# The last 64 rows of w_down: 25 partitions with three rows each in place of 128 half rows

## The chip, the cores and the metric

The kernel runs on one core of a Trainium2 chip. The metric is device time in microseconds (us), the median over runs of the whole program. A profile is one more execution; it has a time of its own and a span, from the first to the last instruction that it records.

## The reference

One token passes through a transformer block: attention over a cache of 4096 positions with 32 heads of 128, then a gated feed-forward layer. Everything is bf16 at the borders.

```python
h  = x + A(layernorm(x))        # q = ln @ wq; softmax(q k^T / sqrt(128)) v; @ wo
g  = ln2 @ w_gate               # ln2 = layernorm(h), 640 -> 1728
u  = ln2 @ w_up
h2 = h + (gelu_tanh(g) * u) @ w_down   # 1728 -> 640
```

The change touches only the last product. 1728 is 13 * 128 + 64, so 13 full slices of 128 rows of `w_down` leave a remainder of 64 rows.

## The kernel before, in words

**Order of work.** A small class `S` collects the instructions of each engine in program order; every engine runs its own list in order, and an instruction waits on semaphores of what it needs. There is no scheduler: the order in the source is the order on the engine. All large transfers are issued by SyncE (SP) on one queue, in source order: `wq`, the K and V caches in 16 pieces of 4 MB, `wo` in two parts, `w_gate`, `w_up`, and last the pieces of `w_down`. So the queue holds work from the start to the end.

**Attention.** Eight groups of four heads: VectorE (DVE) multiplies K by the broadcast q (L329), TensorE (PE) folds the products (L338), DVE and ScalarE (ACT) make the softmax, and PE multiplies by V (L385, and L393 for the last group). The projection by `wo` is L586.

**Feed-forward.** `up` (L632) makes g in PSUM tile `pg` and u in `pu`, each 128 partitions by `NF` = 14 columns. Columns 0 to 12 hold the 13 full slices. Column 13 holds rows 1600 to 1727 on partitions 0 to 127: its upper 64 partitions are the remaining rows 1664 to 1727, its lower 64 repeat rows that are already in another column. DVE and ACT compute the gelu (L639 to L647), and L648 writes `hm`, bf16, 128 by 14.

**The down product.** `w_down` lies in `wd_sb`, by slots of 640 columns. It comes in five transfers, issued in this order: `wdr`, the remainder, into slot 13 (L566); then `wd0` to `wd3` (L571) with 6, 4, 2 and 1 slots, 128 partitions each. Each output of 640 is cut into four quarters, `j`, which are accumulated on four rows (0, 32, 64, 96) of PSUM tile `pd` (shown as `pf` in the profile), so one slot is four matmuls of one column of `hm` (the stationary operand) by 160 columns of `wd_sb` (L664). PE goes through the slots of `wd0`, then slot 13, then `wd1`, `wd2`, `wd3`; before the first matmul of each it waits for that transfer. L668 copies `pd` to SBUF, and L669 stores it.

**The remainder before.** Row r of the 64 is cut in halves: half h lies on partition 2r + h, so slot 13 has 128 partitions of 320 columns. To match this, one matmul (L650) with the selection matrix `twice` copies h of row r to partitions 2r and 2r + 1, and DVE (L652) multiplies by the parity mask `hpar`, which gives two columns `hr`: one is zero on odd partitions, the other on even ones. Quarters 0 and 1 use the first column, quarters 2 and 3 the second. `hpar` and `twice` are made at the start by DVE (L219, L221) from the identity `I32`.

Of the kernel before, what the change touches and what calls it, by code (L numbers as in the profile page):

```python
# [5 lines left out]
FP32 = mybir.dt.float32  # L6
BF16 = mybir.dt.bfloat16
ALU = mybir.AluOpType
ACTF = mybir.ActivationFunctionType
AX = mybir.AxisListType  # L10

D = 640
# [3 lines left out]
DF = 1728  # L16
NC_D = D // 128
# [6 lines left out]
NG = H // HG  # L24
# [9 lines left out]
NFT = 13  # L34
NF = NFT + 1
WD_PARTS = (6, 4, 2, 1)

WD_COLS = []
for _n in WD_PARTS:
    _b = 128 * len(WD_COLS)  # L40
    WD_COLS += [(_b, _n, _i) for _i in range(_n)]
FREM = DF - NFT * 128


class Sched:
# [64 lines left out]
def bass_sequential_preLN__gqa_block_cached__glu_gated_geglu__decode_kernel(  # L110
# [12 lines left out]
    S = Sched(nc)  # L123

    def sb(name, shape, dt):
        return nc.alloc_sbuf_tensor(name, shape, dt)
# [5 lines left out]
    vbuf = [sb("vbuf%d" % i, [128, R, DH], BF16) for i in range(2)]  # L132

    def over(name, base, shape):
        return nc.alloc_sbuf_tensor_at(name, shape, BF16, offset=nc.lookup_mloc(base).addr)
# [2 lines left out]
    wo_sb = over("wo_sb", arena, [128, NW, HW, D])  # L138
    wg_sb = over("wg_sb", kbuf[NG % 2], [128, NC_D, DF])
    wu_sb = over("wu_sb", kbuf[(NG + 1) % 2], [128, NC_D, DF])  # L140
    wd_sb = over("wd_sb", vbuf[NG % 2], [128, NF, D])

    NPR = 3
    prod = [sb("prod%d" % i, [128, RP, DH], BF16) for i in range(NPR)]
# [33 lines left out]
    r_t = sb("r_t", [128, NF], FP32)  # L178
    gu = sb("gu", [128, NF], FP32)
    hm = sb("hm", [128, NF], BF16)  # L180
    hr = sb("hr", [128, 2], BF16)
    hpar = sb("hpar", [128, 2], FP32)
    twice = sb("twice", [128, FREM, 2], BF16)
    o_sb = sb("o_sb", [128, D // 4], BF16)
    hx = sb("hx", [128, 32, NC_D], FP32)
    m32 = sb("m32", [128, 32], FP32)
# [5 lines left out]
    I32 = sb("I32", [128, 128], FP32)  # L192
# [5 lines left out]
    pz = nc.alloc_psum_tensor("pz", [128, 512], FP32)  # L198
# [17 lines left out]

    t_e4 = S.op("vector", lambda v: v.reduce_sum(
        e4[:, :], I32[:, :].rearrange("p (j i) -> p j i", j=4), axis=AX.X), [t_i32])
    S.op("vector", lambda v: v.reduce_sum(  # L219
        hpar[:, :], I32[:, :].rearrange("p (r h) -> p h r", h=2), axis=AX.X))  # L220
    t_tw = S.op("vector", lambda v: v.tensor_copy(  # L221
        twice[:, :, :], I32[:, 128 - FREM:128].unsqueeze(2).to_broadcast([128, FREM, 2])))
    t_m32 = S.op("vector", lambda v: v.reduce_sum(
        m32[:, :], I32[:, :].rearrange("p (j i) -> p i j", j=4), axis=AX.X))
    S.op("vector", lambda v: v.reduce_sum(
# [3 lines left out]
    a = S.op("vector", lambda v: v.reduce_sum(  # L229
        jred[:, :], I32[:, :].rearrange("p (j c) -> p j c", c=HW), axis=AX.X))  # L230
    b = S.op("vector", lambda v: v.reduce_sum(
        cred[:, :], I32[:, :].rearrange("p (j c) -> p c j", c=HW), axis=AX.X))
# [11 lines left out]
    kfree, vfree = [None] * NG, [None] * NG  # L244
# [45 lines left out]
    a = None  # L290
    for c in range(NC_D):
        a = S.op("tensor", lambda t, c=c: t.matmul(
            pm[:, c:c + 1], x_sb[0:1, c::NC_D], ones_bf[0:1, 0:1],
            start=(c == 0), stop=(c == NC_D - 1), skip_group_check=True),
            [d_x, t_onebf], token=(c == NC_D - 1))
# [146 lines left out]
    for n in range(NG - 1):  # L442
        w = (n - 3) // 2 if n >= 3 and n % 2 else None
        p, o = n - 1, n - 2
# [62 lines left out]
    p, o = g - 1, g - 2  # L507
# [45 lines left out]
    def load_wo(lo, hi):  # L553
# [10 lines left out]
    d_wu = pieces("wu", wu_sb, B_w_up[:, :].rearrange("(p c) n -> p c n", c=NC_D),  # L564
                  [0, 5], [kfree[NG - 1]])
    d_wdr = S.dma("sync", "wdr", lambda s: s.dma_start(  # L566
        wd_sb[:, NFT, 0:D // 2], B_w_down[NFT * 128:DF, :].rearrange("r (h n) -> (r h) n", h=2)), [vfree[NG - 2]])
    d_wd = []
    for i, n in enumerate(WD_PARTS):
        s0 = len(d_wd)  # L570
# [1 line left out]
            wd_sb[:, s0:s0 + n, :],  # L572
            B_w_down[128 * s0:128 * (s0 + n), :].rearrange("(p i) n -> p i n", i=n)), [vfree[NG - 2]])
        d_wd += [tok] * n
    d_wd.append(d_wdr)


    pp = pf[0]
# [1 line left out]
    def project(w):  # L580
        tok = None
        for c in range(HW):
            for cc in range(NC_D):
                last = w == NW - 1 and c == HW - 1 and cc == NC_D - 1
                first = w == 0 and c == 0 and cc == 0
                tok = S.op("tensor", lambda t, c=c, cc=cc, first=first, last=last: t.matmul(  # L586
                    pp[:, cc:cc + 1], wo_sb[:, w, c, cc::NC_D], aP[:, w * HW + c:w * HW + c + 1],
                    start=first, stop=last, skip_group_check=True),
                    [t_aP[w], d_wo[w], red_done[NG * NP - 2]], token=last)
        return tok  # L590

    for i in range(w - 1):
# [8 lines left out]
    b = project(w)  # L601
    t_h = S.op("vector", lambda v: v.scalar_tensor_tensor(
        out=h32[:, :], in0=x32[:, :], scalar=1.0, in1=pp[:, 0:NC_D], op0=ALU.mult, op1=ALU.add,
# [4 lines left out]
    NQ = D // 4  # L608
# [13 lines left out]
    def up(ps, w, d_w):  # L622
# [16 lines left out]
    a = S.op("vector", lambda v: v.tensor_copy(g_t[:, :], pg[:, 0:NF]), [t_g])  # L639
    a = S.op("vector", lambda v: v.tensor_mul(t1[:, :], g_t[:, :], g_t[:, :]), [a])  # L640
    a = S.op("vector", lambda v: v.tensor_mul(t2[:, :], t1[:, :], g_t[:, :]), [a])
    a = S.op("vector", lambda v: v.scalar_tensor_tensor(
        out=t3[:, :], in0=t2[:, :], scalar=GELU_C1, in1=g_t[:, :], op0=ALU.mult, op1=ALU.add), [a])
    a = S.op("scalar", lambda a: a.activation(e_t[:, :], t3[:, :], ACTF.Exp, scale=-2.0 * GELU_C0), [a])
    a = S.op("vector", lambda v: v.tensor_scalar(d_t[:, :], e_t[:, :], 1.0, 0.0, ALU.add, ALU.add), [a])
    a = S.op("vector", lambda v: v.reciprocal(r_t[:, :], d_t[:, :]), [a])
    a = S.op("vector", lambda v: v.tensor_mul(gu[:, :], g_t[:, :], r_t[:, :]), [a])  # L647
    t_hm = S.op("vector", lambda v: v.tensor_mul(hm[:, :], gu[:, :], pu[:, 0:NF]), [a, t_u])  # L648

    b = S.op("tensor", lambda t: t.matmul(  # L650
        pz[:, 32:33], twice[:, :, :], hm[:, NFT:NF], start=True, stop=True), [t_hm, t_tw])
    t_hr = S.op("vector", lambda v: v.tensor_tensor(  # L652
        out=hr[:, :], in0=hpar[:, :], in1=pz[:, 32:33].to_broadcast([128, 2]), op=ALU.mult), [b])

    def down(s, j):
        if s == NFT:
            return hr[:, j // 2:j // 2 + 1], wd_sb[:, NFT, j % 2 * NQ:(j % 2 + 1) * NQ]
        return hm[:, s:s + 1], wd_sb[:, s, j * NQ:(j + 1) * NQ]

    order = list(range(WD_PARTS[0])) + [NFT] + list(range(WD_PARTS[0], NFT))  # L660
    for i, s in enumerate(order):
        for j in range(4):
            last = i == NF - 1
            b = S.op("tensor", lambda t, s=s, j=j, last=last: t.matmul(  # L664
                pd[32 * j:32 * j + 1, 0:NQ], *down(s, j),
                start=False, stop=last, skip_group_check=True),
                [t_hr if s == NFT else t_hm, d_wd[s]], token=(last and j == 3))
    t_o = S.op("vector", lambda v: v.tensor_copy(o_sb[:, :], pd[:, 0:NQ]), [b])  # L668
    d_o = S.dma("sync", "out", lambda s: s.dma_start(  # L669
        out[0, 0, :].rearrange("(j i) -> j i", j=4), o_sb[0:128:32, :]), [t_o])  # L670
# [32 lines left out]
```

## Time and profile before

| what | value |
|---|---|
| median of 3 runs | 203.93 us (203.84 to 203.95) |
| the profiled execution | 204.04 us |
| its span | 202.8 us |
| PE busy | 154.4 us (76%) |
| DVE busy | 116.0 us (57%) |
| read from HBM | 84.23 MB, 415 GB/s over the span |
| share of the 16 DMA engines' time in the main queue | 97.2% |
| `hm` ready (end of L648) | 198.15 us |
| first and last matmul of the down product begin | 198.32 and 200.41 us |
| copy of the result begins (L668) | 200.77 us |

Times inside the execution are microseconds from the start of its span. The trace also holds, for each transfer, the landing records: a transfer over 128 partitions runs on all 16 DMA engines, and each engine reports its own share by one increment of the transfer's semaphore. And it holds the packets, with start, duration and size, though not the number of the DMA engine that carried each.

### The profile page before, as it was taken

The page shows a single profiled execution, that of the slowest core. Times are in us where ns is not written, and L with a number is a line of the kernel's source. Part 1 is how long each engine was busy: PE and PEld are TensorE (multiplying, and loading weights), DVE is VectorE, ACT ScalarE, POOL GpSimd, SP SyncE. Part 2 cuts the span into 40 slices and gives each one's busy share as a digit, 9 for nine tenths or more (in the row PEclk, how much of TensorE's full clock was granted, in tenths as well). Part 3 has the DMA queues.
Part 4 walks back from the last instruction along what each step waited for, and adds up shares of the span by engine and source line. Part 5 has one row for each costly group of instructions (what it writes and reads, how often), then busy time and mean ns, then how long its engine had stood idle before and what let it go on. Part 6 is the DMA issues. An engine that isn't in the chain of part 4 may idle for free.

```text
span 202.8 us, 2488 instructions
## 1 busy us (share of the span) xinstructions
PE 154.4 (76%) x1074; PEld 71.5 (35%) x1080; DVE 116.0 (57%) x150; ACT 30.6 (15%) x110; POOL 1.2 (1%) x7
## 2 busy tenths in 40 slices
PE   1005348689959967998899499959876999988685
PEld 1001013233324322442343134313422344587483
DVE  6100087998099628883993599268899524311121
ACT  2002200006003300240060006000602204000000
POOL 1000000000000000000000000000000000000000
PEclk9999999999999996999999999988999999975555
DMA  7999999999999999999999999999999999999992
GB/s 251 444 436 414 414 472 452 414 420 414 436 465 433 420 409 420 449 448 420 433 414 427 456 427 433 427 414 433 459 427 430 387 424 468 433 393 430 410 404 85
DMA packets 4020, 84.38 MB, mean 416 GB/s; under 512 B 425, under 2 KB 682, under 8 KB 1066
## 3 DMA queue, kind: packets, MB, share of 16 engines
q1 hardware_dynamic: 4008, 84.23, 97.2%
q8 instruction: 8, 0.13, 0.3%
q14 instruction: 2, 0.02, 0.0%
q10 hardware_dynamic: 2, 0.00, 0.0%
HBM read 84.23 MB, written 0.00 MB: 415 GB/s over the span
## 4 chain that ended last, share of the span: by engine, by line
DMA 58%; DVE 24%; PE 15%; SPq 1%; issue 1%
DMA kbuf<-in_A_k_cache_dram 47%; DVE prod L329 17%; DMA wd_sb<-in_B_w_down_dram 11%; PE pf L338 6%; PE pg L385 4%; DVE sc L345 4%; PE pu L385 4%; DVE xz L402 2%; DVE xm L399 1%; SPq L571 0%; DVE mx L353 0%; PE pf L664 0%; DVE mrow L362 0%; PE pm L357 0%; SPq L237 0%
## 5 line engine op out<-in xcount | busy, mean ns | idle before, releaser
L329 DVE TENSOR_TENSOR prod<-kbuf,qb 128x4096 bf16<-128x4096 bf16 x32 | 72.8, 2278 | 46.6 <-DMA kbuf<-in_A_k_cache_dram 46.6
L338 PE MATMUL pf<-prod,Ibf 128*128 128x512 bf16 x256 | 66.0, 405 | 24.4 <-DVE prod L329 24.4
L338 PEld LDWEIGHTS pf<-prod,Ibf 128*128 128x128 bf16 x256 | 24.2, 103 | 63.2 <-DVE prod L329 31.0
L385 PE MATMUL pg<-vbuf,P 128*16 128x512 bf16 x128 | 30.0, 379 | 0.0
L345 DVE TENSOR_REDUCE sc<-pf 128x32 f32<-128x512 f32 x32 | 21.7, 677 | 4.7 <-PE pf L338 4.7
L385 PE MATMUL pu<-vbuf,P 128*16 128x512 bf16 x96 | 22.2, 379 | 0.0
L308 PE MATMUL pq<-wq_sb,xb 128*128 128x512 bf16 x34 | 10.8, 451 | 13.6 <-DMA wq_sb<-in_A_wq_dram 11.6
L370 ACT ACTIVATE nb<-pm 128x4 f32<-128x4 f32 x8 | 1.4, 173 | 119.7 <-PE pm L367 119.7
L374 ACT ACTIVATE P<-sc,nb 32x128 bf16<-32x128 f32 x32 | 18.5, 578 | 0.9
L385 PEld LDWEIGHTS pg<-vbuf,P 128*16 128x16 bf16 x128 | 10.6, 89 | 14.5 <-issue 1.3
L385 PEld LDWEIGHTS pu<-vbuf,P 128*16 128x16 bf16 x96 | 8.1, 90 | 11.7 <-issue 1.7
L314 ACT CAST qb<-pq 32x128 bf16<-32x128 f32 x32 | 8.2, 256 | 16.3 <-PE pq L308 15.6
L308 PEld LDWEIGHTS pq<-wq_sb,xb 128*128 128x128 bf16 x40 | 3.8, 110 | 17.6 <-issue 13.3
L374 ACT ACTIVATION_READ_ACCUMULATOR P<-sc,nb 32x1 f32 x32 | 8.0, 251 | 0.0
L586 PE MATMUL pf<-aP,wo_sb 128*128 128x1 bf16 x160 | 7.0, 178 | 1.3 <-issue 1.0
L586 PEld LDWEIGHTS pf<-aP,wo_sb 128*128 128x128 bf16 x160 | 6.8, 131 | 1.9 <-issue 1.5
L402 DVE TENSOR_REDUCE xz<-xm 16x128 f32<-16x512 f32 x7 | 7.3, 1038 | 0.2
L399 DVE TENSOR_TENSOR xm<-pg,rmask 16x512 f32<-16x512 f32 x4 | 2.7, 671 | 3.4 <-PE pg L385 3.4
L393 PE MATMUL pq<-P,vbuf 128*128 128x4 bf16 x128 | 3.6, 166 | 0.6 <-DMA vbuf<-in_A_v_cache_dram 0.6
L283 ACT ACTIVATE ln<-pz,ln 128x1 f32<-128x1 f32 x2 | 0.5, 261 | 23.2 <-DVE ln L280 23.2
L399 DVE TENSOR_TENSOR xm<-pu,rmask 16x512 f32<-16x512 f32 x3 | 1.9, 644 | 3.2 <-PE pu L385 3.2
L393 PEld LDWEIGHTS pq<-P,vbuf 128*128 128x128 bf16 x128 | 3.5, 104 | 0.7 <-DMA vbuf<-in_A_v_cache_dram 0.7
(80 smaller groups left out, 56.1 us busy)
## 6 DMA issues: line engine op xcount, KB each, us to landing
kbuf<-in_A_k_cache_dram SPq DMA_DIRECT2D x8, 4096.0 KB, 25.1
vbuf<-in_A_v_cache_dram SPq DMA_DIRECT2D x8, 4096.0 KB, 22.7
wq_sb<-in_A_wq_dram SPq DMA_DIRECT2D x1, 5120.0 KB, 15.4
wo_sb<-in_A_wo_dram SPq DMA_DIRECT2D x1, 3840.0 KB, 27.2
wg_sb<-in_B_w_gate_dram SPq DMA_DIRECT2D x1, 2160.0 KB, 21.5
wu_sb<-in_B_w_up_dram SPq DMA_DIRECT2D x1, 2160.0 KB, 26.2
wo_sb<-in_A_wo_dram SPq DMA_DIRECT2D x1, 1280.0 KB, 16.8
wd_sb<-in_B_w_down_dram SPq DMA_DIRECT2D x1, 960.0 KB, 21.4
```

The costliest lines, as they stand in the source:

```text
L308: tok = S.op("tensor", lambda t, c=c, n0=n0: t.matmul(pq[:, :], xb[:, c, :], wq_sb[:, c, n0:n0 + HG * DH], start=(c == 0), stop=(c == NC_D ...
L314: t_qb[g] = S.op("scalar", lambda a, lo=lo, hi=hi, hh=hh: a.copy(qb[lo:hi, g, :], pq[lo:hi, hh * DH:(hh + 1) * DH]), [tok])
L329: return S.op("vector", lambda v: v.tensor_tensor(out=prod[n % NPR][:, :, :], in0=kbuf[g % 2][:, s * RP:(s + 1) * RP, :], in1=qb[:, g, :]. ...
L338: fold_done[n] = S.op("tensor", lambda t, j=j: t.matmul(pf[n % 2][:, :], Ibf[:, :], prod[n % NPR][:, :, j * W:(j + 1) * W], start=(j == 0) ...
L345: red_done[n] = S.op("vector", lambda v: v.reduce_sum(sc[g % 2][:, s * RP:(s + 1) * RP], pf[n % 2][:, :].rearrange("p (r w) -> p r w", r=R ...
L370: e = S.op("scalar", lambda a: a.activation(nb[:, g * HG:(g + 1) * HG], pm[:, 256:256 + HG], ACTF.Copy, scale=-SCALE), [d])
L374: t_exp[g] = S.op("scalar", lambda a, lo=lo, hi=hi, h=h, hh=hh: a.activation(P4[g % 2][lo:hi, :, hh], sc[g % 2][lo:hi, :], ACTF.Exp, bias= ...
L385: t_pv[g] = S.op("tensor", lambda t, i=i, r=r, last=last: t.matmul(pv[g % 2][0:VM, :], P4[g % 2][:, r:r + VR, :], vbuf[g % 2][:, r:r + VR, :],
L393: t_pv[g] = S.op("tensor", lambda t, r=r: t.matmul(pq[:, 0:HG], vbuf[g % 2][:, r, :], P4[g % 2][:, r, :], start=(r == 0), stop=(r == R - 1 ...
L399: a = S.op("vector", lambda v: v.tensor_tensor(out=xm[:, :, :], in0=pv[g % 2][0:VM, :].rearrange("p (r d) -> p r d", r=VR), in1=rmask[:, : ...
L402: t_ext[g] = S.op("vector", lambda v: v.reduce_sum(xz[g % 2][:, :], xm[:, :, :].rearrange("p r d -> p d r"), axis=AX.X), [a, t_acc[g - 2] ...
L586: tok = S.op("tensor", lambda t, c=c, cc=cc, first=first, last=last: t.matmul(pp[:, cc:cc + 1], wo_sb[:, w, c, cc::NC_D], aP[:, w * HW + c ...
```

## The change

The remainder is now read as 75 whole rows, 1653 to 1727, with three rows of 640 columns on each of 25 partitions; rows 1653 to 1663 are read a second time, and their h is set to zero. `wd_sb` has 16 slots, 13 to 15 being the remainder. `hq` is column 13 of `hm` spread over three columns by the mask `hcol` (1 where the row's place among the 75, modulo 3, is the column's number, and 0 on the lower 64 partitions); one matmul with the selection matrix `hrow` sums it to 25 partitions by three columns, and DVE copies that to `hr`. PE goes through the slots of `wd0` and `wd1`, then 13 to 15, then `wd2` and `wd3`.

```diff
+NRP = 25
+NRR = 3
+ROFF = 128 - NRP * NRR
...
-    S.op("vector", lambda v: v.reduce_sum(
-        hpar[:, :], I32[:, :].rearrange("p (r h) -> p h r", h=2), axis=AX.X))
-    t_tw = S.op("vector", lambda v: v.tensor_copy(
-        twice[:, :, :], I32[:, 128 - FREM:128].unsqueeze(2).to_broadcast([128, FREM, 2])))
+    hsum = hx[:, 0:NRP // NC_D, :]
+    t_hsum = S.op("vector", lambda v: v.reduce_sum(
+        hsum, I32[:, ROFF:128].rearrange("p (a b i) -> p a b i", b=NC_D, i=NRR), axis=AX.X))
+    t_hrow = S.op("vector", lambda v: v.memset(hrow[:, :], 0.0))
+    t_hrow = S.op("vector", lambda v: v.tensor_copy(
+        hrow[:, 0:NRP].rearrange("p (a b) -> p a b", b=NC_D), hsum), [t_hsum, t_hrow])
+    t_hcol = S.op("vector", lambda v: v.reduce_sum(
+        hcol[:, :], I32[:, ROFF:128].rearrange("p (r i) -> p i r", i=NRR), axis=AX.X))
+    t_hcol = S.op("vector", lambda v: v.memset(hcol[0:128 - FREM, :], 0.0), [t_hcol])
...
     d_wdr = S.dma("sync", "wdr", lambda s: s.dma_start(
-        wd_sb[:, NFT, 0:D // 2], B_w_down[NFT * 128:DF, :].rearrange("r (h n) -> (r h) n", h=2)), [vfree[NG - 2]])
+        wd_sb[0:NRP, NFT:NFT + NRR, :],
+        B_w_down[DF - NRP * NRR:DF, :].rearrange("(p i) n -> p i n", i=NRR)), [vfree[NG - 2]])
...
+    a = S.op("vector", lambda v: v.tensor_tensor(
+        out=hq[:, :], in0=hcol[:, :], in1=hm[:, NFT:NF].to_broadcast([128, NRR]), op=ALU.mult), [t_hm, t_hcol])
     b = S.op("tensor", lambda t: t.matmul(
-        pz[:, 32:33], twice[:, :, :], hm[:, NFT:NF], start=True, stop=True), [t_hm, t_tw])
-    t_hr = S.op("vector", lambda v: v.tensor_tensor(
-        out=hr[:, :], in0=hpar[:, :], in1=pz[:, 32:33].to_broadcast([128, 2]), op=ALU.mult), [b])
+        pz[:, 32:32 + NRR], hrow[:, :], hq[:, :], start=True, stop=True), [a, t_hrow])
+    t_hr = S.op("vector", lambda v: v.tensor_copy(hr[:, :], pz[:, 32:32 + NRR]), [b])

     def down(s, j):
-        if s == NFT:
-            return hr[:, j // 2:j // 2 + 1], wd_sb[:, NFT, j % 2 * NQ:(j % 2 + 1) * NQ]
+        if s >= NFT:
+            return hr[0:NRP, s - NFT:s - NFT + 1], wd_sb[0:NRP, s, j * NQ:(j + 1) * NQ]
         return hm[:, s:s + 1], wd_sb[:, s, j * NQ:(j + 1) * NQ]

-    order = list(range(WD_PARTS[0])) + [NFT] + list(range(WD_PARTS[0], NFT))
+    n = sum(WD_PARTS[0:2])
+    order = list(range(n)) + list(range(NFT, NFT + NRR)) + list(range(n, NFT))
```

More of the change, by code (lines that the diff above doesn't have):

```diff
@@ L140, in bass_sequential_preLN__gqa_block_cached__glu_gated_geglu__decode_kernel @@
     wu_sb = over("wu_sb", kbuf[(NG + 1) % 2], [128, NC_D, DF])
-    wd_sb = over("wd_sb", vbuf[NG % 2], [128, NF, D])
+    wd_sb = over("wd_sb", vbuf[NG % 2], [128, NFT + NRR, D])
     NPR = 3
@@ L180, in bass_sequential_preLN__gqa_block_cached__glu_gated_geglu__decode_kernel @@
     hm = sb("hm", [128, NF], BF16)
-    hr = sb("hr", [128, 2], BF16)
-    hpar = sb("hpar", [128, 2], FP32)
-    twice = sb("twice", [128, FREM, 2], BF16)
+    hq = sb("hq", [128, NRR], BF16)
+    hr = sb("hr", [128, NRR], BF16)
+    hcol = sb("hcol", [128, NRR], FP32)
+    hrow = sb("hrow", [128, 128], BF16)
     o_sb = sb("o_sb", [128, D // 4], BF16)
@@ L574, in bass_sequential_preLN__gqa_block_cached__glu_gated_geglu__decode_kernel @@
         d_wd += [tok] * n
-    d_wd.append(d_wdr)
+    d_wd += [d_wdr] * NRR
     pp = pf[0]
@@ L648, in bass_sequential_preLN__gqa_block_cached__glu_gated_geglu__decode_kernel @@
     t_hm = S.op("vector", lambda v: v.tensor_mul(hm[:, :], gu[:, :], pu[:, 0:NF]), [a, t_u])
+    a = S.op("vector", lambda v: v.tensor_tensor(
+        out=hq[:, :], in0=hcol[:, :], in1=hm[:, NFT:NF].to_broadcast([128, NRR]), op=ALU.mult), [t_hm, t_hcol])
     b = S.op("tensor", lambda t: t.matmul(
-        pz[:, 32:33], twice[:, :, :], hm[:, NFT:NF], start=True, stop=True), [t_hm, t_tw])
-    t_hr = S.op("vector", lambda v: v.tensor_tensor(
-        out=hr[:, :], in0=hpar[:, :], in1=pz[:, 32:33].to_broadcast([128, 2]), op=ALU.mult), [b])
+        pz[:, 32:32 + NRR], hrow[:, :], hq[:, :], start=True, stop=True), [a, t_hrow])
+    t_hr = S.op("vector", lambda v: v.tensor_copy(hr[:, :], pz[:, 32:32 + NRR]), [b])
     def down(s, j):
-        if s == NFT:
-            return hr[:, j // 2:j // 2 + 1], wd_sb[:, NFT, j % 2 * NQ:(j % 2 + 1) * NQ]
+        if s >= NFT:
+            return hr[0:NRP, s - NFT:s - NFT + 1], wd_sb[0:NRP, s, j * NQ:(j + 1) * NQ]
         return hm[:, s:s + 1], wd_sb[:, s, j * NQ:(j + 1) * NQ]
-    order = list(range(WD_PARTS[0])) + [NFT] + list(range(WD_PARTS[0], NFT))
+    n = sum(WD_PARTS[0:2])
+    order = list(range(n)) + list(range(NFT, NFT + NRR)) + list(range(n, NFT))
     for i, s in enumerate(order):
         for j in range(4):
-            last = i == NF - 1
+            last = i == len(order) - 1
             b = S.op("tensor", lambda t, s=s, j=j, last=last: t.matmul(
@@ L666, in bass_sequential_preLN__gqa_block_cached__glu_gated_geglu__decode_kernel @@
                 start=False, stop=last, skip_group_check=True),
-                [t_hr if s == NFT else t_hm, d_wd[s]], token=(last and j == 3))
+                [t_hr if s >= NFT else t_hm, d_wd[s]], token=(last and j == 3))
     t_o = S.op("vector", lambda v: v.tensor_copy(o_sb[:, :], pd[:, 0:NQ]), [b])
```

## The prediction

> **What bounds the kernel now.** I read the page's slices and queues first, then the end of the chain of waits, then the timeline of the last five microseconds, then DMA in that window.
>
> ```profile
> PEclk9999999999999996999999999988999999975555
> DMA  7999999999999999999999999999999999999992
> q8 instruction: 8, 0.13, 0.3%
> ```
>
> DMA is full in all slices but the first and last: the kernel is a stream of weights and cache, and what counts is when its last bytes land and what follows. PE's granted clock is 0.5 in the last four slices. The eight instruction packets of q8 matter below.
>
> ```profile
> 176.66 0.43 SPq L571
> 177.09 0.04 issue
> 177.13 22.85 DMA wd_sb<-in_B_w_down_dram
> 199.99 0.04 issue
> 200.03 0.71 PE pf L664 x9
> ```
>
> The chain ends in `wd2` landing at 199.99 and the last matmuls. In the timeline, the last waits:
>
> ```profile
> 197.98 0.17 DVE L648 TENSOR_TENSOR hm<-gu,pu 128x14 bf16<-128x14 f32 x1 [1.80 <-PE pu L632]
> 198.20 0.10 PEld L650 LDWEIGHTS pz<-hm,twice 128*128 128x128 bf16 x1 [0.42 <-DVE hm L648]
> 198.32 0.97 PE L664 MATMUL pf<-wd_sb,hm 128*1 128x160 bf16 x24
> 199.08 0.34 PE L664 MATMUL pf<-wd_sb,hr 128*1 128x160 bf16 x4
> 199.21 1.50 PE L664 MATMUL pf<-wd_sb,hm 128*1 128x160 bf16 x28
> 200.03 0.10 PEld L664 LDWEIGHTS pf<-wd_sb,hm 128*1 128x1 bf16 x8 [0.41 <-DMA wd_sb<-in_B_w_down_dram]
> 200.41 0.09 PEld L664 LDWEIGHTS pf<-wd_sb,hm 128*1 128x1 bf16 x4 [0.28 <-DMA wd_sb<-in_B_w_down_dram]
> ```
>
> PE idles twice, for `wd2` and for `wd3` (which landed at 200.37); everything after 200.41 (four matmuls, copy, store) is fixed. So a single number decides: when the last four matmuls can begin. It is the later of the last share of `wd3` and of PE's own queue.
>
> **The landing.** Stretching 195 to 203 us into 40 slices of 0.2 us shows that the 16 engines do not end together:
>
> ```profile
> DMA  9899899889999989665543100000000000000000
> ```
>
> The landing records of `wd3` give each engine's end: 198.35, .40, .47, .57, .58, .75, .97, then 199.35, .47, .72, .82, .88, .93, .95, 200.13 and 200.37. In the packet records an engine runs its packets back to back (each starts within some 10 ns of another's end, so that 16 chains can be followed), and it gets the same share of every transfer, so a delay stays: a q8 packet of 16 KB holds one engine for 1.02 to 1.10 us, its next packet is about 0.5 us slow, and each time another engine is hit. Seven of the nine late engines carry such a hit.
>
> **The change, part by part.**
>
> *Removed from the queue:* `wdr` before is 8 packets of 640 B on each of 16 engines; its landings stand 0.20 to 0.23 us behind those of `w_up`, engine by engine. That goes from every engine that gets no share of the new one: 0.21.
>
> *Added:* 25 packets of 3840 B (25 contiguous pieces on both sides). Packets of 2560 and 5120 B take 0.102 and 0.198 us here, so one takes 0.15. How 25 packets spread isn't shown. In every transfer of this trace the engines used carry equal shares (128 partitions: 8 packets on each of 16; the store of 4 partitions: one packet and one completion on each of four; `x_sb`: one packet). Equal shares of 25 mean five engines with five packets, 0.73 us, net +0.50 on these; the other end, all on one, is 25 × 0.15, net +3.4; below, two packets on each of 13 engines, net +0.07. I take five, the only even split that uses several engines.
>
> *The landing then:* the last engine that isn't one of the five ends at 200.37 − 0.21 = 200.16. One of the five ends 0.50 later than in the list. Those at 199.47 or less become harmless (199.97); 199.95 becomes 200.45, 200.13 becomes 200.63, 200.37 becomes 200.87.
>
> The trace's rows alone do not say which five. [...] No row shows an engine's number.
>
> *PE's queue.* A slot is four matmuls; slots follow each other by 0.134 us (199.08 to 199.21 above), and the six slots of `wd0` with their faster start take 0.76 (198.32 to 199.08).
> - The new DVE multiply `hq` stands between `hm` and the selection matmul, and all 64 down matmuls are queued behind that on PE. L652, its like, takes 0.16, and dependent DVE steps start 0.04 after each other's end: +0.21 (0.16 to 0.28). PE begins the slots at 198.53 instead of 198.32.
> - One slot becomes three: 2 × 0.134 = +0.27. The matmuls have 25 rows instead of 128 but the same 160 columns; no row of this stage has so few, but L292's matmuls of one row still take 0.17 where L650's with 128 rows takes 0.19. I take the same price; the low end is nothing for all three, −0.40.
> - Order: `wd0` to 199.29, `wd1` (landing at 199.17 or earlier) four slots to 199.83, remainder three to 200.23, `wd2` two, and the last slot begins at 198.53 + 0.76 + 9 × 0.134 = 200.49.
> - Moving the remainder behind `wd1` costs nothing: both are present, so PE is simply busy. The copy to `hr` (0.16 after the matmul, 198.8) is one us early. The former cover, 0.40 us of waits, is used up: 0.48 added.
>
> *Free:* five DVE steps replace two (0.27 and 0.22) at 2 us, about 0.5 more. They delay `xb`, ready at 6.43, which isn't needed until `wq` lands at 16.15. SP's issue is one DMA for one. The 14 KB read twice are in the packets above.
>
> **Sum.** The last slot can begin at 200.49 by PE instead of 200.41: +0.08. On the profiled execution that makes 204.12; on the median of the runs, 0.11 below it, 204.01. The gain of 0.21 in landing is there but PE hides it.
>
> **The rivals.**
> 1. *A late engine is among the five* (slower). If it is the one at 200.37, the last slot begins at 200.87 + 0.04 = 200.91: +0.50, 204.43. If the worst is the one at 200.13: 200.67, +0.26, 204.19. It decides from a landing of 199.95 upward. For it: nine of 16 are late, and with any five of 16 the worst is included in 5 of 16. Against: `x_sb`'s only packet (1.91 to 1.97 us) was served by an engine whose first `wq` packet starts just after it, at 1.975 or 1.980; both chains of packets fitting that run among the early ones until 160 us. [...]
> 2. *PE isn't late* (gain): the three short slots cost little, so landing decides: 200.16 + 0.04 = 200.20, −0.21, 203.72. For it: only 25 rows. Against: in the rows, spacing follows the 160 columns.
> 3. *The transfer does not spread:* all 25 packets on one engine that ends between 198.35 and 200.37: last landing 201.7 to 203.8, so +1.4 to +3.4, 205.3 to 207.3.
>
> **How the numbers follow.** About 0.2%, 0.41 us, is what a measurement of this kernel can tell from no change, so 203.52 to 204.34 counts as the same. Forecast, +0.08: 0.58. Rival 1: 0.20 for +0.50 and 0.11 for about +0.26 (still the same). Rival 2: 0.07, of which 0.02 for a little more than it says. Rival 3: 0.04. So same is 0.58 + 0.11 + 0.05 = 0.74, slower 0.20 + 0.04 = 0.24, faster 0.02. The range takes rival 2's end (203.72), and rival 1's (204.43) with 0.1 for the spread of runs and the upper price of `hq`: 203.72 to 204.55. The forecast's own range is 203.9 to 204.15.
>
> **What would show it.** Right: PE runs 16 slots in one row from 198.53 without a wait for DMA, the last at 200.49; the last share of `wd3` at 200.16; five landings in `wdr`'s records, 0.73 behind those of `w_up`. Wrong: PE still waiting for `wd3` at 200.4 or later (rival 1); matmuls of the remainder closer than 0.134 a slot (rival 2); one landing of `wdr` near 197 (rival 3). I am wrong altogether if the delays of the engines, by start or by instruction packets, fall on other engines than in this trace.

## The result, and the profile after

The changed kernel takes 204.70 us (median of 6 runs, 204.50 to 205.29), the one before 203.92 (6 runs, 203.77 to 203.97): slower, by a ratio of 1.0044 with a 95% interval of 1.0031 to 1.0057. The profiled execution took 204.84 against 204.04, so its difference, 0.80, is that of the medians, 0.78.

The end of the chain of waits after (start, duration, what):

```profile
167.69 27.85 DMA wu_sb<-in_B_w_up_dram
195.54 0.05 issue
195.59 2.77 PE pu L642 x70
...
198.45 0.18 DVE hm L658
198.63 0.02 issue
198.65 0.18 DVE hq L660
198.83 0.05 issue
198.88 0.19 PE pz L662
199.06 2.45 PE pf L676 x61
201.52 0.02 issue
201.54 0.33 DVE o_sb L680
```

Before, the chain ended in the landing of `w_down`. Now it ends in that of `w_up`, at 195.54 instead of 195.06, and after that nothing waits for a transfer any more: it is PE, DVE, PE. Until shortly before that the two executions agree: `w_gate`, the transfer ahead of `w_up`, has its last landing at 189.90 before and at 189.95 after.

The weight loads of the last slots (PEld) and the matmuls (PE):

```profile
198.99 1.16 PEld L676 LDWEIGHTS pf<-wd_sb,hm 128*1 128x1 bf16 x40
200.42 0.22 PEld L676 LDWEIGHTS pf<-wd_sb,hr 25*1 25x1 bf16 x12 [0.27 <-issue]
200.92 0.23 PEld L676 LDWEIGHTS pf<-wd_sb,hm 128*1 128x1 bf16 x12 [0.27 <-issue]
198.99 1.50 PE L676 MATMUL pf<-wd_sb,hm 128*1 128x160 bf16 x40
200.43 0.56 PE L676 MATMUL pf<-wd_sb,hr 25*1 25x160 bf16 x12
200.92 0.57 PE L676 MATMUL pf<-wd_sb,hm 128*1 128x160 bf16 x12
```

No wait for DMA, as forecast, but two idle stretches of 0.27 in the weight loads, one at each change of the row count. The last slot begins at 201.14 instead of 200.41: 0.73 later, in three parts. `hm` ends 0.47 later (198.62 instead of 198.15). From there to the first slot it takes 0.37 instead of 0.17. From the first slot to the last it takes 2.15 instead of 2.09, though the waits for `wd2` and `wd3` are gone. The copy of the result begins 0.77 later, 201.54 instead of 200.77.

Why `w_up` lands late shows in the stretches from 193 to 195 us; the last columns are PE's clock, the DMA share and GB/s. Before, then after:

```profile
193.00:194.00 1.00, 1.00 (x31) 1.00 (x30) 0.00 (x0) 0.00 (x0) 0.00 (x0) 0.50 0.91 368
194.00:195.00 1.00, 0.40 (x12) 0.32 (x10) 0.49 (x3) 0.00 (x0) 0.00 (x0) 0.50 1.02 407
```

```profile
193.00:194.00 1.00, 0.64 (x19) 0.55 (x16) 0.29 (x2) 0.00 (x0) 0.00 (x0) 0.50 1.09 328
194.00:195.00 1.00, 0.00 (x0) 0.00 (x0) 0.62 (x5) 0.21 (x1) 0.00 (x0) 0.50 0.80 248
```

The DMA engines are about as busy as before, yet move 288 GB/s instead of 388. Over 2 us that is 200 KB, and 200 KB at 416 GB/s (the mean rate of before) are 0.48 us, as much as the delay of `w_up`. The agreement is rough: over 192 to 196 us the same view has 350 instead of 390 GB/s, which makes 0.38 us. It is there in the packet records too. A 17280-byte packet of `w_up` takes 0.644 us and a 7680-byte packet of `wd0` 0.292; from 192 to 196 us over 70 packets are longer than usual for their size, `w_up`'s by up to 0.6, `wd0`'s by up to 0.23 and the remainder's own by up to 0.15. Nor are only a few engines late: taken in order, all 16 landings of `wd3` come later than before, by 0.28 to 1.06 us. Below, **slow** is this sum: what packets that start from 192 to 196 us take beyond the usual time of their size, where that is over 0.02 us. It is 0.6 us before (one packet behind an instruction packet, and a few of `wdr`) and 8.8 us after.

### The profile page after: what moved, and what is told of

Same layout as the page of the kernel before. It is cut to its first block, busy times and chain, and to the rows that moved or that the text cites. A ratio compares the mean times of both kernels' runs of the same rounds, so it can differ in the third digit from the quotient of the medians.

```text
span 203.6 us, 2515 instructions
## 1 busy us (share of the span) xinstructions
PE 156.0 (77%) x1088; PEld 72.3 (35%) x1088; DVE 116.5 (57%) x154; ACT 30.6 (15%) x110; POOL 1.2 (1%) x7
## 4 chain that ended last, share of the span: by engine, by line
DMA 60%; DVE 28%; PE 10%; issue 1%; SPq 0%; DVEq 0%
DMA kbuf<-in_A_k_cache_dram 46%; DVE prod L338 19%; DMA wu_sb<-in_B_w_up_dram 14%; DVE sc L354 4%; PE pf L347 4%; PE pu L394 3%; DVE xz L411 2%; PE pu L642 1%; DVE xm L408 1%; PE pf L676 1%; DVE mx L362 1%; DVE mrow L371 0%; SPq L246 0%; DVE o_sb L680 0%; PE pm L366 0%
## 5 line engine op out<-in xcount | busy, mean ns | idle before, releaser
L317 PE MATMUL pq<-wq_sb,xb 128*128 128x512 bf16 x40 | 12.1, 442 | 12.3 <-DMA wq_sb<-in_A_wq_dram 11.1
L642 PE MATMUL pu<-hln,wu_sb 128*128 128x1 bf16 x70 | 2.8, 176 | 1.9 <-DMA wu_sb<-in_B_w_up_dram 1.9
L292 ACT ACTIVATE ln<-pz,ln 128x1 f32<-128x1 f32 x2 | 0.5, 262 | 24.1 <-DVE ln L289 24.1
```

Source lines behind the costliest of these rows:

```text
L317: tok = S.op("tensor", lambda t, c=c, n0=n0: t.matmul(pq[:, :], xb[:, c, :], wq_sb[:, c, n0:n0 + HG * DH], start=(c == 0), stop=(c == NC_D ...
L642: b = S.op("tensor", lambda t, s=s, c=c, part=part, first=first, last=last: t.matmul(ps[:, s:s + 1], part, hln[:, c:c + 1], start=first, s ...
```

## The experiments

The runs were taken in four groups. The kernels of a group ran on one chip and share the runs of the kernel before, whose median was 204.01, 203.97, 203.98 and 203.92 in the four. Medians follow; the last four columns are from the one profiled execution of each kernel. "Last slot" is when the last four matmuls begin.

| run | us | against before | `w_up` lands | `hm` ends | last slot | slow, us |
|---|---|---|---|---|---|---|
| before | 203.92 | | 195.06 | 198.15 | 200.41 | 0.6 |
| changed | 204.70 | +0.78 | 195.54 | 198.62 | 201.14 | 8.8 |
| transfer_alone | 204.47 | +0.46 | 195.50 | 198.59 | 200.69 | 10.3 |
| compute_alone | 204.38 | +0.37 | 195.57 | 198.65 | 201.18 | 0.5 |
| rows128 | 204.50 | +0.49 | 195.52 | 198.60 | 200.93 | 10.8 |
| spread16 | 204.54 | +0.53 | 195.29 | 198.37 | 200.75 | 8.4 |
| no_transfer | 204.27 | +0.30 | 194.86 | 197.95 | 200.47 | 0.5 |
| step4 | 203.91 | −0.06 | 195.08 | 198.16 | 200.42 | 0.5 |
| whole_rows128 | 204.17 | +0.20 | 195.33 | 198.41 | 200.89 | 0.6 |
| last_in_queue | 204.59 | +0.62 | 195.10 | 198.18 | 200.91 | 0.5 |
| five_step5 | 204.08 | +0.10 | 195.25 | 198.34 | 200.40 | 5.4 |
| crowd_at_64 (one run) | 204.65 | +0.67 | 195.75 | 198.83 | 200.92 | 14.8 |
| halves_on_five | 204.19 | +0.21 | 195.27 | 198.35 | 200.41 | 4.6 |
| step2 | 205.11 | +1.19 | 195.30 | 198.39 | 200.67 | 9.3 |

### Parting the change in two: transfer_alone and compute_alone

```diff
 # transfer_alone: before, with
+        wd_sb[0:25, NFT:NFT + 3, :], B_w_down[DF - 75:DF, :].rearrange("(p i) n -> p i n", i=3)
-            return hr[:, j // 2:j // 2 + 1], wd_sb[:, NFT, j % 2 * NQ:(j % 2 + 1) * NQ]
+            return hr[:, j // 2:j // 2 + 1], wd_sb[:, 5, j % 2 * NQ:(j % 2 + 1) * NQ]
 # compute_alone: changed, with the half rows of before, and
-            return hr[...], wd_sb[0:NRP, s, j * NQ:(j + 1) * NQ]
+            return hr[...], wd_sb[0:NRP, NFT, j % 2 * NQ:(j % 2 + 1) * NQ]
```

> The kernel before, with only the transfer of the remainder as 25 partitions of three rows; PE's order and instructions are those of before, and slot 13's four matmuls read data of slot 5 instead, so the remainder's share of the result is left out. Theory A (the transfer on five engines holds up the stream while the tail of w_up is still landing): w_up lands at about 195.5 as in the changed kernel (195.54), not at 195.06; hm ends at 198.6; the last slot begins at about 200.65 (14 slots from 198.8, or the last landing at 200.65); time 204.2. Theory B (the late landing of w_up has nothing to do with the transfer; it is chance, or comes with the new instructions): w_up at 195.0 to 195.1, time 203.7 to 204.0.

Measured: 204.47, ratio 1.0023 (1.0012 to 1.0033), above theory A's 204.2. The disturbance is A's: `w_up` lands at 195.50 with 10.3 us of slow packets. The same stretches in this run:

```profile
193.00:194.00 1.00, 0.39 (x12) 0.30 (x10) 0.51 (x3) 0.00 (x0) 0.00 (x0) 0.50 0.78 234
194.00:195.00 1.00, 0.00 (x0) 0.00 (x0) 0.62 (x5) 0.21 (x1) 0.00 (x0) 0.50 1.02 321
```

But the late start of PE's list isn't what costs here, since PE still waits for `wd2` and `wd3`:

```profile
200.29 0.10 PEld L665 LDWEIGHTS pf<-wd_sb,hm 128*1 128x1 bf16 x8 [0.25 <-DMA wd_sb<-in_B_w_down_dram]
200.69 0.09 PEld L665 LDWEIGHTS pf<-wd_sb,hm 128*1 128x1 bf16 x4 [0.29 <-DMA wd_sb<-in_B_w_down_dram]
```

From its first slot at 198.76, PE's list alone would reach the last one at 198.76 + 0.76 + 7 × 0.134 = 200.46. It begins at 200.69 because `wd3` lands at 200.65 instead of 200.37: the slow packets make everything behind them late too. That is +0.28 for the last slot; the profiled execution is 0.40 longer and the median 0.46, and the rest was not followed.

> The changed kernel with the old transfer (128 half rows); its three remainder slots read those 25 partitions of slot 13, so the remainder's share of the result is wrong in value, but every instruction is there. Theory A: w_up lands at 195.06, and only PE's queue is longer: hq 0.21, two more slots 0.27, and two changes of the row count at 0.14 each that the changed kernel's timeline shows, less 0.40 of former waits: the last slot at 200.65 to 200.7, time 204.2. Theory B: the PE side or the code itself carries all of the 0.78, w_up lands late here too, time 204.6 to 204.7.

Measured: 204.38, ratio 1.0019 (1.0007 to 1.0030), with runs from 204.04 to 205.18. No slow packets. The profiled execution, at 204.85, is not a typical one: one engine landed the last part of `wo` at 185.26, 0.77 after the next, 8 us ahead of anything that the change touches; `w_up` has its last landing at 195.57 and the next at 195.11. PE's list takes what the changed kernel's takes (2.15 from the first slot to the last). So by the medians the transfer is worth 0.46 and the PE side 0.37; together they make 0.83, where the change measures 0.78. That they add up is partly chance. In the traces the last slot comes 0.28 later in transfer_alone, and here by about 0.31 (an estimate, with `w_up` at 195.11): each alone is partly covered by the waits of before. Only together do they use the cover up, and the last slot comes 0.73 later.

### The PE side: rows128 and no_transfer

```diff
 # rows128: changed, with
-            return hr[0:NRP, ...], wd_sb[0:NRP, s, j * NQ:(j + 1) * NQ]
+            return hr[:, ...], wd_sb[:, s - NFT, j * NQ:(j + 1) * NQ]
 # no_transfer: changed, with d_wdr = None, and
+            return hr[0:NRP, ...], wd_sb[0:NRP, s - NFT, j * NQ:(j + 1) * NQ]
```

> The changed kernel, but its twelve remainder matmuls take 128 rows (the columns of hr on all partitions, against slots 0 to 2 of w_down, so the remainder's share of the result is wrong in value). If the change from 128 to 25 rows and back costs the two gaps of 0.27 instead of 0.134: no gap, the last slot 0.2 to 0.28 earlier than in the changed kernel, time 204.45. If the gaps come from something else (a wait, the instruction fetch at 198.2): the same 204.7.

Measured: 204.50 (1.0017, 1.0006 to 1.0028), 0.20 under the changed kernel's median, though that was taken in another group of runs. The idle stretches are gone:

```profile
198.97 1.16 PEld L676 LDWEIGHTS pf<-wd_sb,hm 128*1 128x1 bf16 x40
200.13 0.40 PEld L676 LDWEIGHTS pf<-wd_sb,hr 128*1 128x1 bf16 x12
200.53 0.40 PEld L676 LDWEIGHTS pf<-wd_sb,hm 128*1 128x1 bf16 x12
```

From the first slot (198.97) to the last (200.93) it takes 1.96 instead of 2.15; the slot distance of 0.134 and the prediction's 0.76 + 9 × 0.134 = 1.97 hold. So going from 128 rows to 25 and back costs 0.19. In the changed kernel a slot begins 0.28 and 0.27 after the one before it at the two changes, instead of 0.134, and the slot after each follows 0.09 behind, which wins a part back.

> The changed kernel without any transfer of the remainder; its twelve matmuls read rows of slots 0 to 2 of w_down instead, so the remainder's share of the result is wrong in value. In the four kernels so far that send the remainder to 25 or 32 partitions, packets of all engines are slow between 192.5 and 195.1 us and w_up lands at 195.3 to 195.5; in the two with 128 partitions it isn't so. Theory A (the writes into few partitions slow the others): no slow packets, w_up at 195.0 to 195.1, last slot near 200.7 by PE's queue alone, time 204.2. Theory C (what slows is that engines without a share run ahead into w_down while others still read w_up): slow packets as before, w_up at 195.4, time 204.6.

Measured: 204.27 (1.0017, 1.0008 to 1.0026): theory A, with no slow packets beyond those of before. Engines that run ahead into `w_down` did no harm here (0.5 us). PE decides alone: its list begins at 198.32 and takes 2.15. (That `w_up` lands 0.20 earlier than before isn't the work of the missing transfer: the last part of `wo`, 10 us ahead, is 0.18 early already. With `hm` at 198.15 the last slot would come at 200.67, +0.26, close to the measured 0.30.)

### Which part of the transfer slows the stream

```diff
 # spread16: changed, with NRP = 32, NRR = 2 (64 rows, partitions 0..31)
 # the others: transfer_alone, with the destination
 # step4:         wd_sb[0:128:4, NFT:NFT + 2, :]   64 rows, two per partition
 # step2:         wd_sb[0:64:2,  NFT:NFT + 2, :]   64 rows, two per partition
 # five_step5:    wd_sb[0:125:5, NFT:NFT + 3, :]   75 rows, three per partition
 # crowd_at_64:   wd_sb[64:89,   NFT:NFT + 3, :]   75 rows, three per partition
 # whole_rows128: wd_sb[:, NFT, :]                 128 rows, one per partition
```

> The changed kernel with the 64 remaining rows as two rows on each of 32 partitions (no row twice), which divides over 16 engines: two packets of 2560 B each. Theory A: nothing is concentrated, w_up lands at 195.06 as before; PE has 15 slots and the two changes of row count: the last slot at 200.5 to 200.55, time 204.05. If few destination partitions and not few engines hold up the stream: w_up late again, time 204.5. Theory B, as a matter of the code: 204.5.

Measured: 204.54 (1.0037, 1.0016 to 1.0058), with 8.4 us of slow packets although all 16 engines have equal shares. So few engines were not needed for the harm; theory A in its first form (five engines) falls here. The runs scatter upward, to 206.71.

> As transfer_alone (PE as before, the remainder's share left out), but the 64 rows go as two rows to each of 32 partitions that lie four apart, 0, 4, ... 124, so that no part of the partitions is crowded. Theory A1 (crowding: 25 or 32 neighbouring partitions must take what 16 engines bring besides their own): slow packets gone or far fewer, w_up at 195.1, time 203.9 to 204.0. Theory A2 (any transfer whose engines write into partitions that other engines write at the same time): slow packets as in spread16 (8 us in sum), w_up at 195.3, time 204.3 to 204.4.

Measured: 203.91, ratio 0.9992 (0.9973 to 1.0011), no difference. The same bytes as spread16, in the same packets, on as many partitions and engines, but on partitions four apart: no slow packets beyond those of before, and the landings of before. A1's forecast holds.

```profile
193.00:194.00 1.00, 0.82 (x24) 0.73 (x22) 0.14 (x1) 0.00 (x0) 0.00 (x0) 0.50 0.94 397
194.00:195.00 1.00, 0.00 (x0) 0.00 (x0) 0.61 (x5) 0.21 (x1) 0.00 (x0) 0.50 0.88 364
```

> As step4 (two rows on each of 32 partitions, 16 engines, PE as before, the remainder's share left out), but on partitions 0, 2, ... 62: none are neighbours, yet all lie in the lower half. If what crowds is a group of partitions that shares a way in, and the upper half has ways of its own: twice the load of step4 on half the ways, as in spread16, which had 8 us of slow packets; slow packets of 4 to 8 us, w_up at 195.2 to 195.3, time 204.2 to 204.5. If only direct neighbours matter: as step4, no slow packets, w_up at 195.08, time 203.9.

Measured: 9.3 us of slow packets, `w_up` at 195.30, and a time above either forecast: 205.11, ratio 1.0047 (1.0022 to 1.0073), runs from 204.24 to 206.32. The profiled execution, 204.31, shows the mechanism, not what the slowest runs add; that stays open. Its stretches:

```profile
193.00:194.00 1.00, 0.21 (x8) 0.12 (x5) 0.65 (x4) 0.00 (x0) 0.00 (x0) 0.50 0.96 324
194.00:195.00 1.00, 0.00 (x0) 0.00 (x0) 0.64 (x4) 0.21 (x1) 0.00 (x0) 0.50 1.01 312
```

No two of these partitions are neighbours, so direct neighbours weren't needed for it. What differs from step4 is only which 32 partitions: every second one below 64, not every fourth one of all 128.

> As transfer_alone, but on partitions 64 to 88. A1: crowding is crowding; slow packets of 8 us in sum between 192.5 and 195.1, w_up at 195.3 to 195.5, hm at 198.5. If only the first partitions are special: no slow packets, w_up at 195.06.

Measured in one run: 204.65, 14.8 us of slow packets, `w_up` at 195.75. Partitions 64 to 88 crowd as well. The last slot, 200.92, again follows `wd3` (200.87).

> As transfer_alone (75 rows, three on each of 25 partitions, five engines; PE as before, the remainder's share left out), but the 25 partitions are 0, 5, ... 120. It parts the two things that the change does to the transfer: five engines, and neighbouring partitions. Theory A1 (crowding of neighbouring partitions slows everyone): no slow packets, w_up at 195.06, hm at 198.15; the five engines land 0.5 later, the others 0.21 earlier, so time 203.7 to 203.8 if the five are early ones (last_in_queue's five landings, 199.33 to 200.25, say so), 204.0 to 204.4 if one of the last is among them. Rival (five engines alone slow the stream): 8 us of slow packets again, w_up at 195.5, 204.4.

Measured: 204.08, ratio 0.9995 (0.9978 to 1.0011), undecided. Neither theory alone: spread over all partitions, five engines still leave 5.4 us of slow packets, half of the crowded form's, and `w_up` lands at 195.25. `wd3` lands at 200.36, so the lighter share that the other engines carry doesn't show in the last landing.

> As transfer_alone (PE as before, the remainder's share left out), but the transfer brings the last 128 rows whole, one on each partition: twice the bytes, packets of 1280 B. Theory A in both forms: no slow packets, since all partitions take part as in every other load; each engine spends 8 x 0.055 = 0.44 instead of 0.22 us, w_up at 195.06, wd3 lands at 200.6, time 204.15. If larger packets of the remainder by themselves slow the stream: slow packets, w_up late, 204.4 or more.

Measured: 204.17, ratio 1.0017 (0.9998 to 1.0036), as expected in time: twice the bytes of before in packets of 1280 B and no slow packets beyond those of before. (`w_up` lands at 195.33 in this profile, but on one engine; the next has it at 195.02.) The size of the remainder's packets isn't it.

### Two attempts to keep the idea: last_in_queue and halves_on_five

```diff
 # last_in_queue: changed, with the transfer of wdr issued after wd3, and
-    n = sum(WD_PARTS[0:2])
+    n = NFT
 # halves_on_five: before, with half = the 128 half rows, and
+    d_wdr: wd_sb[0:125, NFT, 0:D // 2] <- half[0:125, :]
+    d_wdq: wd_sb[125:128, NFT, 0:D // 2] <- half[125:128, :]
 # and slot 13 waits for both
```

> The changed kernel with the remainder's transfer issued after wd3 and its three slots last on PE; the whole result is computed. Theory A: w_up is undisturbed at 195.06, hm ends at 198.15; thirteen slots run from 198.53 to 200.22; what the transfer then slows is only wd2 and wd3 on late engines. The remainder's five shares land 0.75 to 1.0 after wd3 on the same engines, which the landings of the changed kernel spread over early and late ones (194.17 to 195.60): the last at about 201.0, so the last slot at 201.3 to 201.4 and time 204.8 to 204.95. If the five were the early ones: last slot 200.7, 204.2.

Measured: 204.59 (1.0036, 1.0020 to 1.0052). `w_up` lands at 195.10, undisturbed, and the five shares at 199.33, .36, .37, .96 and 200.25, so the five engines were early ones. But now the slow packets (2.7 us, from 197 to 200 us) are those of `wd2`, `wd3` and the remainder itself; `wd3` lands at 200.41, and the remainder's slots come after it:

```profile
198.56 2.20 PE L676 MATMUL pf<-wd_sb,hm 128*1 128x160 bf16 x52
200.69 0.57 PE L676 MATMUL pf<-wd_sb,hr 25*1 25x160 bf16 x12
```

The disturbance went where the transfer went.

> The kernel before, its half rows kept and PE unchanged, but the transfer of the 128 half rows is cut into one of 125 partitions (125 is 5 times 25, so five engines by equal shares) and one of the last 3. The result is complete. Theory A1: all partitions take part, 25 packets of 640 B on each of five engines, 0.7 to 0.8 us, net +0.5 there, and 0.21 less on the others but three; no slow packets; w_up at 195.06, wd3 lands at 200.16 if the five are early ones, last slot 200.20, time 203.7: faster than both kernels by 0.1% or more. If one of the five is late: last landing 200.5 to 200.9, 204.1 to 204.4. If each engine's own 25 neighbouring partitions crowd as well: w_up late, 204.4.

Measured: 204.19, ratio 1.0006 (0.9989 to 1.0023), so not the gain that was hoped for. 4.6 us of slow packets bring `w_up` to 195.27, PE starts its slots at 198.52 instead of 198.32, and it still waits for `wd3`, which lands at 200.37 as before: what the other engines are spared doesn't reach the last landing. No version tried beats the kernel before.

## Why the prediction was wrong, step by step

The forecast was +0.08 us, 204.01, with a range of 203.72 to 204.55; measured were +0.78 and 204.70.

**The step that failed** is "*The landing then*": the transfer was priced on its own five engines only (+0.50 there, 0.21 less elsewhere), and on `w_down` only. So the last share of `wd3` was put at 200.16, and `hm` at 198.15 went into the sum as a constant. Measured were 200.65 and 198.62. `w_up` is issued ahead of the remainder, but the engines are not in step: before the change the first one ends its share of `w_up` at 193.01 and the last at 195.06. So early ones already write the remainder while late ones still bring `w_up`: in the changed kernel the remainder's 25 packets start from 192.48 to 194.48, and `w_up` lands from 192.96 to 195.54. Sent to 25 neighbouring partitions, it comes with slower packets around it (8.8 us in sum instead of 0.6), `w_up` lands 0.48 late, and `hm` with it. No rival had this mechanism. With PE as before it costs 0.46, there by way of the late `wd3` (transfer_alone); with PE's longer list, which has no wait left, the delay of `hm` counts in full. Of two transfers of the same 64 rows in the same packets, the one to every fourth partition costs nothing (step4), and the one to every second partition below 64 has 9.3 us of slow packets (step2: +0.26 for the last slot of its trace, +1.19 in the median).

Where the partitions lie counts: 32 partitions all below 64 have 8.4 (spread16) and 9.3 us (step2) of slow packets, and 32 over all 128 have 0.5, none beyond the usual (step4). It isn't the whole account: the partitions of five_step5 and halves_on_five reach over all 128 too, yet they have 5.4 and 4.6 us.

**A mis-sized term:** the remainder's three slots. Two extra slots at 0.134 were right (rows128: 1.96 for the whole list, 1.97 forecast), but changing the row count and changing it back cost 0.19 more. The prediction priced such matmuls by L292's duration, where the price lies in the switch. With 128 rows throughout, the two gaps of 0.27 are gone (rows128); what PE does in them no run shows.

**Right:**
- `hq` costs 0.20, forecast 0.21: from the end of `hm` to the first slot 0.37 instead of 0.17.
- The 0.40 of waits was cover, and it is used up: PE runs all slots without waiting.
- Five engines: the semaphore of `wdr` shows six records, one at 175.06 and five landings from 194.17 to 195.60. (Five packets of 0.15 make 0.75, not the 0.73 of the prediction; its sum doesn't depend on it.)
- The five setup steps make `xb` ready 0.45 later (6.88 instead of 6.43), far ahead of `wq` (16.06); the moved order costs nothing by itself.

**The sum with what was measured:** 0.08 as predicted, 0.47 for `hm` and 0.19 for the row counts make 0.74; the last slot came 0.73 later.

**Rival 1** had the right sign and two thirds of the size (+0.50), for the wrong reason. The last landing, 200.65, is long before the last slot at 201.14, and in last_in_queue the five engines were early ones, as the `x_sb` packet had hinted. Its path, PE waiting for a late `wd3`, is the one that decides in transfer_alone, but there all engines are late and not only five.

**Open:** what the slow packets wait for, and why five engines spread over all partitions still do half the harm. One reading was not tested: that harm is done where an engine writes partitions that another engine is filling. In a transfer over 128 partitions each of the 16 engines brings 8 packets, and in halves_on_five each of the five brings 25, so they can't have kept to 8 partitions of their own; in step4 all 16 may have. The packets carry no number of their engine, so which writes meet can't be read. Why the runs of step2 and spread16 scatter up to 206.32 and 206.71 wasn't followed either.

## What to carry to other kernels

Look at the rate of the whole stream around a small transfer, not only at its own bytes. Here, before the change, the engines ended `w_up` up to 2 us apart (193.01 to 195.06), and the 25 packets of the remainder, queued behind it, came with a delay of 0.48 us in its last landing. Of the transfers tried, only those that were spread over all 128 partitions and carried by all 16 engines brought no slow packets beyond the usual (0.6 us before, 0.5 in step4, 0.6 in whole_rows128); with only one of the two it was 4.6 us or more (halves_on_five 4.6, five_step5 5.4, spread16 8.4, step2 9.3). And before a step is added on an engine that waits for transfers, count its waits as a budget: here 0.40 us, less than what two extra slots, one DVE step and a change of row count cost.

## What the hardware showed that was not expected

- 82 KB to 32 partitions out of the first 64 came with 8.4 (spread16) and 9.3 us (step2) of longer packets in sum, 0.5 to 0.6 us for each of the 16 engines; the same 82 KB to every fourth of the 128 cost nothing that shows (step4: 0.5 us, 0.6 before).
- The transfer to 25 partitions marked its semaphore once at 175.06, long before its first packet (192.48), and then five times, from 194.17 to 195.60.
- In the changed kernel a change between matmuls of 128 and 25 rows put 0.28 and 0.27 us between the starts of two slots, where a slot of the same kind follows in 0.134; there and back it cost 0.19 in all (2.15 us from the first slot to the last, 1.96 in rows128).
